# A list scheduler for everything ahead of the first exponential of a transformer layer

## The chip, the cores and the metric

The kernel runs on one core of a Trainium2 chip. The metric is the device time of one execution in microseconds; the value of a kernel is the median of its runs. Profiles show one execution each.

## The reference

The layer takes x (2048 rows of 512, f32), normalises its rows and adds three things: x itself, an attention block, and a dense block with a gelu.

```python
xn = layernorm(x)                                # rows of 512, eps 1e-5
qkv = (xn @ wqkv)                                # 512 x 1536; 32 heads of 16
p = softmax(q k^T * 16 ** -0.5)                  # 2048 x 2048 for each head
attention = (p @ v) @ wo
h = gelu(xn @ w1 + b1)                           # 512 x 1792
out = x + attention + h @ w2 + b2
```

## The kernel before, in words

Dense operands are carried as two f16 parts (a high part and the remainder of it), so that a product of 512 summands is twelve matmuls: four chunks of 128, each as high x high, high x low and low x high. The parts of a weight are made after scaling by a power of two, which needs the largest size of its entries: `scales` makes it from column maxima (or from absolute sums taken on ScalarE with `accum_out`) by a transpose, a row maximum, a broadcast matmul and a few small VectorE operations. This is called measuring a weight here. `w1`, `w2`, `wo` and the query and key columns of the later heads are loaded in pieces of 512 KB into the three buffers `wch` to be measured, and most of them loaded a second time later to be split.

The heads are worked in 8 groups of four. Queries and keys of a group are stored in DRAM (`qk_d`) from the tile `stg` and come back as stacks `qst` and `kst`, one for each block of 512 rows (four blocks), pair of heads and role; `stacks` issues the loads. Row block t of a group (32 row blocks in all) is 16 units. In each unit `s_half` computes four score tiles of 128 x 512 (matmuls into a PSUM bank `pS`, then `reduce_max` on VectorE, line 258); after 16 units the maxima go out to DRAM and come back as two more rows of the query stack (`s_end`, `store`). `LEAD` = 19 units later `e_half` computes the transposed scores with the maxima already subtracted (`pT`) and the exponential on ScalarE (line 303), and `v_half` multiplies by the values `vv` (`pV`). So the first exponential can only come when 19 score units are done: 16 for the first row block and three more. Beside the attention, `dense` fills TensorE with all other products (`pD`).

The loop over units (`unit`) starts from position `pos` and writes the order of every engine by hand (`manual_schedule`). Its work and the tail behind it are the same in both kernels. What lies ahead of it, the prologue, is in the kernel before written as generators that are advanced by hand: `stats` (row statistics and normalisation of four row tiles of x), `transpose_x` (transposes and the two f16 parts `xt`), `prep_qk` and `prep_v` (measuring and splitting the weights of head group 0..3 and of the values), `project` (queries or keys of four groups for one block of rows), `v_tiles` (the values of the first `NV` = 8 row tiles), `measure` (18 pieces, two of them by VectorE maxima at line 741, sixteen by absolute sums at line 857) and `tile_and_unit` (one unit of scores with some products of `v_tiles` between the halves). Only TensorE's order is fixed by hand there, from the transposes of the second block of x on; VectorE, ScalarE and the transfer queue (SP, which issues all DMAs) get the order of the program. The units 16 to 18 run in the loop already, with `LFILL` = (8, 16, 12) products of value tiles in place of the exponentials. Matmuls on a zeroed tile (`warm`, line 890) run at the start. `dbank` gives the dense products their PSUM bank; until unit `LEAD` it takes from the banks of `pT`.

PSUM has eight banks: three for scores (S), three for transposed scores (T), one for dense products (D), one for values (V). In the prologue transposes, projections and value tiles take turns on T, D, V and S.

After the prologue `rest` gives the dense work of the first stage (the remaining value tiles, then the projections of the other heads as soon as their weights are split), and `prepare` is advanced once in each unit: it ends the measuring (a reduction over the bias `b1_s`, the maxima over `am_all` and `amx`), and has the weights split on GpSimd.

Of the kernel before, what the change touches and what calls it, by code (L numbers as in the profile page):

```python
# [36 lines left out]
LFILL = (8, 16, 12)  # L37
WARM = (14, 3, 2, 2)
NV = 8
# [11 lines left out]
def layer_kernel(ctx: ExitStack, tc: tile.TileContext, x, wqkv, wo, w1, b1, w2, b2, out):  # L51
# [31 lines left out]
    def clear(i):  # L83
        for b in range(NQB):
# [120 lines left out]

    mt_of, ptiles, pv_of, stores = {}, {}, {}, {}
# [39 lines left out]
    def s_half(u, n):  # L246
# [4 lines left out]
        if t not in mt_of:  # L251
            mt_of[t] = work.tile([P, 4, 4, 4], F32, name="mt", bufs=2)
        ks, qs = kst[g % 2], qst[g % 2]
        p, a = divmod(n, 2)
        r = slice(64 * a, 64 * a + 62)
        s = banks("S")
        tiled(None, s, qs[p][qb][r, qt * P:(qt + 1) * P], ks[p][kb][r, :], True, True)
        nc.vector.reduce_max(mt_of[t][:, n, qt, kb:kb + 1], s, axis=AX.X)  # L258
        given("dve", 600)

# [145 lines left out]
    def dbank():  # L406
        turn[0] += 1
        if pos[0] < LEAD:
            return banks("T"), None
        return hold("D", "T")  # L410
# [46 lines left out]
    def split_qk(m, wf, inv, ready_w):  # L457
        wh = ph.tile([P, 2, 2, NC, P], F16, name="wqk_h", bufs=2)
        for w in (1, 0):
            split_pool(wh[:, w, 0], wh[:, w, 1], wf[w], inv[:, 8 + 2 * m + w:9 + 2 * m + w])  # L460
# [5 lines left out]
    def prep_qk(m, wf, bank, ready_w):  # L466
        am = work.tile([P, 2], F32, name="am_qk", bufs=2)
        for w in range(2):
            nc.vector.tensor_reduce(am[:, w:w + 1], wf[w], axis=AX.XY, op=ALU.max, apply_absolute_value=True)
            yield  # L470
        box = []
        yield from scales(am, 2, bank, box)
        inv, fac = box
        wh = ph.tile([P, 2, 2, NC, P], F16, name="wqk_h", bufs=2)
        for w in (1, 0):
            (split if w and m == 0 else split_pool)(wh[:, w, 0], wh[:, w, 1], wf[w], inv[:, w:w + 1])
            yield
        nc.vector.tensor_tensor(sexp[:, m:m + 1], fac[:, 0:1], fac[:, 1:2], op=ALU.mult)
        nc.vector.tensor_scalar_mul(sexp[:, m:m + 1], sexp[:, m:m + 1], DH ** -0.5)
        ready_w[m] = wh  # L480
# [179 lines left out]
    def unit(gen):  # L660
# [4 lines left out]
        if e >= 0 and e % (2 * NQB * 16) == 0 and e < NU:  # L665
            fetch_scale(e // (2 * NQB * 16))
        if u == LEAD and cur[0] is not None:
            burst(gen, cur[0].left())
        pos[0] += 1
        for a in range(2):  # L670
# [7 lines left out]
            if u < LEAD:  # L678
                burst(gen, LFILL[u - 16] // 2)
# [36 lines left out]
    with ExitStack() as st1:  # L716
# [6 lines left out]
        def load_x(t):  # L723
            xs[t] = px.tile([P, D], F32, name="xs", bufs=8)
            nc.sync.dma_start(xs[t], x[t * P:(t + 1) * P, :])

        def pin(i):
            if loads and not pos[0]:
                tc.keep_in_program_order(i)

        def chunk(src):
            wf = ph.tile([P, 4 * W], F32, name="wch", bufs=3)
            v = wf.rearrange("p (a b) -> p a b", b=src.shape[2])
            if len(loads) <= NM:
                pin(nc.sync.dma_start(v, src))
            else:
                later(2, lambda: nc.sync.dma_start(v, src), True)
            return v

        def absmax(dst, v):  # L740
            nc.vector.tensor_reduce(dst, v, axis=AX.XY if len(v.shape) == 3 else AX.X, op=ALU.max,
                                    apply_absolute_value=True)
            given("dve", 600)
# [11 lines left out]
        am_all = work.tile([P, 16], F32, name="am_all")  # L755
        fac1, inv1 = [], []

        def fetch(k):
            while len(loads) <= min(k + (1 if pos[0] else 2), NM + 15):
# [3 lines left out]
        for t in range(4):  # L763
            load_x(t)
        wfs.append(load_qk(0))
        for t in range(4, 8):
            load_x(t)
        wvv = wqkv[:, 2 * D:3 * D].rearrange("(c p) n -> p c n", p=P)
        loads = []
        wvf = [chunk(wvv[:, :, i * W:(i + 1) * W]) for i in range(2)]  # L770
        wvh = [ph.tile([P, NC, D], F16, name="wvh", tag="wsp", bufs=3) for _ in range(2)]
        fac_v, ready_w = [], {}

        def stats(sb):
            mv = work.tile([P, 4, nc.vector.BN_AGGR_DIM], F32, name="mv", bufs=2)
            for i in range(4):
                bs = work.tile([P, nc.vector.BN_STATS_DIM], F32, name="bs", bufs=2)
                nc.vector.bn_stats(bs, xs[4 * sb + i])
                yield
                nc.vector.bn_aggr(mv[:, i, :], bs)  # L780
            sd = work.tile([P, 5, 4], F32, name="sd", bufs=2)
            nc.vector.tensor_scalar_add(sd[:, 0], mv[:, :, 1], 1e-5)
            nc.scalar.activation(sd[:, 1], sd[:, 0], AF.Sqrt)
            yield

            nc.vector.tensor_scalar_mul(sd[:, 4], mv[:, :, 0], -1.0)
            nc.vector.tensor_tensor(sd[:, 2], sd[:, 1], sd[:, 1], op=ALU.mult)
            yield
            nc.vector.tensor_tensor(sd[:, 2], sd[:, 2], sd[:, 0], op=ALU.add)
            yield  # L790
            nc.vector.reciprocal(sd[:, 3], sd[:, 2])
            yield
            nc.vector.scalar_tensor_tensor(sd[:, 2], sd[:, 1], 2.0, sd[:, 3], op0=ALU.mult, op1=ALU.mult)
            yield
            for i in range(4):
                v = xs[4 * sb + i]
                if sb and i >= 2:
                    nc.scalar.activation(v, v, AF.Identity, bias=sd[:, 4, i:i + 1])
                    nc.scalar.activation(v, v, AF.Copy, scale=sd[:, 2, i:i + 1])
                else:  # L800
                    nc.vector.tensor_scalar(v, v, mv[:, i, 0:1], sd[:, 2, i:i + 1], op0=ALU.subtract, op1=ALU.mult)
                yield

        free = ["T", "D", "T", "V", "T", "S", "S"]

        def vbank():
            turn[0] += 1
            return banks(free[turn[0] % len(free)])

        def transpose_x(sb, c):  # L810
            cs = slice(sb * QB, (sb + 1) * QB)
            pt = vbank()
            for i in range(4):
                nc.tensor.transpose(pt[:, i * P:(i + 1) * P], xs[4 * sb + i][:, c * P:(c + 1) * P], ident)
            nc.scalar.activation(xt[:, 0, c, cs], pt, AF.Copy)
            if sb and c % 2:
                pf = ph.tile([P, QB], F32, name="pf", bufs=2)
                nc.scalar.activation(pf, pt, AF.Copy)
                nc.gpsimd.tensor_tensor(xt[:, 1, c, cs], pf, xt[:, 0, c, cs], op=ALU.subtract)
            else:  # L820
                nc.vector.tensor_tensor(xt[:, 1, c, cs], pt, xt[:, 0, c, cs], op=ALU.subtract)
            if c == NC - 1:
                for t in range(4 * sb + 8, min(4 * sb + 12, NT)):
                    load_x(t)

        def prep_v():
            am = work.tile([P, 3], F32, name="am_v")
            for i in range(2):
                junk = ph.tile([P, 4 * W], F32, name="wch", bufs=3)
                tc.keep_in_program_order(nc.scalar.activation(junk.rearrange("p (a b) -> p a b", b=W), wvf[i], AF.Abs,  # L830
                                                              scale=1.0 / SPREAD, accum_out=am[:, i:i + 1]))
                yield
            nc.vector.tensor_tensor(am[:, 2:3], am[:, 0:1], am[:, 1:2], op=ALU.max)
            box = []
            yield from scales(am[:, 2:3], 1, sbank, box)
            inv, fac = box
            fac_v.append(fac)
            for i in range(2):
                cs = slice(i * W, (i + 1) * W)
                split(wvh[0][:, :, cs], wvh[1][:, :, cs], wvf[i], inv[:, 0:1])  # L840

        def some(gen, n):
            for _ in range(n):
                next(gen, None)

        def measure():

            for w in range(2):
                v = fetch(w)
                for m in (2, 3):  # L850
                    absmax(am_all[:, 8 + 2 * m + w:9 + 2 * m + w], v[:, :, (m - 2) * P:(m - 1) * P])
                absmax(am_all[:, 10 + w:11 + w], wfs[1][w])
                yield
            for n in range(16):
                v = fetch(2 + n)
# [441 lines left out]
```

## Time and profile before

| what | us |
|---|---|
| median of three runs (lowest, highest) | 1510.72 (1508.43, 1512.08) |
| the profiled execution | 1512.14 |
| its span | 1510.4 |
| first score matmul, from the span's start | 38.80 |
| first exponential | 110.15 |
| TensorE, VectorE, ScalarE, GpSimd busy | 1479.5, 1385.1, 1258.9, 661.4 |

The page of the profile gives the busy time of each engine over the span. PE is TensorE, PEld its weight loads, DVE is VectorE, ACT is ScalarE, POOL is GpSimd, SP the queue that issues the transfers. In rows of the timeline stand the start, the length, the engine, the line of the kernel, the operation, the tile written and the tiles read, the count, and in brackets the idle time ahead of it with what ended that. In groups stand the count, busy time, mean in ns, and the idle time ahead of them by releaser. The chain of waits follows the work that ended last back to what released it.

### The profile page before, as it was taken

What the parts mean: (1) busy time and instruction counts of PE and PEld (TensorE: products, weight loads), DVE (VectorE), ACT (ScalarE), POOL (GpSimd) and SP (SyncE); (2) the same over time, 40 slices, a digit from 0 to 9 for tenths busy, and PEclk for the clock granted to TensorE, in tenths of its full rate; (3) what the DMA queues carried; (4) which work ended last, traced back from release to release, by engine and by line L of the source; (5) the groups of instructions that cost most, each with busy time, mean ns of one, the idle gap of its engine ahead of it and who ended that gap; (6) DMA issues with size and microseconds to landing.
All of it is one profiled execution on the core that took longest, in us unless ns stands there. A gap on an engine that the chain in (4) does not pass through costs nothing.

```text
span 1510.4 us, 87999 instructions
## 1 busy us (share of the span) xinstructions
PE 1479.5 (98%) x40052; PEld 820.6 (54%) x40052; DVE 1385.1 (92%) x2317; ACT 1258.9 (83%) x2351; POOL 661.4 (44%) x685
## 2 busy tenths in 40 slices
PE   7999999999999999999999999999999999999998
PEld 3435555555555555555555555555555555555553
DVE  7889998999899999999999999999999999999923
ACT  5548887888899888899988889998889999888884
POOL 3101879433577411268731137873104877211210
PEclk8999999999999999999999999999999999999999
DMA  7650676323322310131112211131111210111432
GB/s 227 182 182 26 206 236 208 109 75 104 88 75 74 91 50 29 40 79 43 50 40 58 53 43 41 42 85 57 29 34 53 70 43 20 50 53 39 131 97 93
DMA packets 114414, 124.82 MB, mean 83 GB/s; under 512 B 24700, under 2 KB 86012, under 8 KB 114040
## 3 DMA queue, kind: packets, MB, share of 16 engines
q1 hardware_dynamic: 114040, 119.19, 26.5%
q8 instruction: 313, 5.13, 1.4%
q14 instruction: 61, 0.50, 0.1%
HBM read 81.66 MB, written 37.34 MB: 79 GB/s over the span
## 4 chain that ended last, share of the span: by engine, by line
PE 78%; DVE 9%; DMA 4%; POOL 4%; SPq 2%; issue 1%; ACT 1%; DVEq 0%; POOLq 0%; ACTq 0%
PE pV L167 23%; PE pD L167 21%; PE pT L167 17%; PE pS L167 16%; DVE mt L258 8%; POOL wsp L1005 1%; DMA wch<-in_B_w_dram 1%; DMA qk_d<-stg 1%; POOL wch L1003 1%; DMA m_d<-mhl 1%; DMA wq<-in_A_wqkv_dram 1%; POOL wsp L1004 1%; SPq L402 1%; PE pT L436 0%; POOL stg L518 0%
## 5 line engine op out<-in xcount | busy, mean ns | idle before, releaser
L258 DVE TENSOR_REDUCE mt<-pS 128x1 f32<-128x512 f32 x2048 | 1307.4, 684 | 50.2 <-PE pS L167 30.5
L303 ACT ACTIVATE pe<-pT 128x512 f32<-128x512 f32 x2048 | 1111.9, 599 | 180.9 <-PE pT L167 77.3
L167 PE MATMUL pV<-pe,vv 64*32 64x512 f32 x8192 | 1077.9, 595 | 0.1
L167 PE MATMUL pT<-qst,kst 64*32 64x512 f16 x8192 | 714.3, 378 | 5.7 <-DMA qst<-m_d 4.2
L167 PE MATMUL pS<-kst,qst 62*32 62x512 f16 x8192 | 625.1, 379 | 7.3 <-DVE mt L258 4.7
L167 PEld LDWEIGHTS <-qst 62*32 62x32 f16 x8192 | 281.1, 92 | 226.5 <-issue 59.4
L167 PEld LDWEIGHTS <-kst 64*32 64x32 f16 x8192 | 280.7, 91 | 178.4 <-issue 77.3
L167 PE MATMUL pD<-xb,wc 64*32 64x512 f16 x5376 | 362.2, 378 | 0.0
L167 PE MATMUL pD<-w_s,g 64*32 64x512 f16 x5376 | 359.4, 377 | 0.0
L167 PEld LDWEIGHTS pV<-pe,vv 64*32 64x32 f32 x8192 | 183.4, 105 | 88.5 <-PE pV L167 2.9
L167 PE MATMUL pD<-xt,wqk_h 64*32 64x512 f16 x2304 | 152.2, 378 | 0.1
L167 PEld LDWEIGHTS <-wc 64*32 64x32 f16 x5376 | 117.6, 92 | 42.9 <-issue 0.6
L167 PEld LDWEIGHTS <-g 64*32 64x32 f16 x5376 | 113.3, 92 | 43.8
L1139 POOL TENSOR_TENSOR xa<-xa,yt 128x512 f32<-128x512 f32 x16 | 20.4, 1278 | 242.0 <-ACT yt L1137 241.9
L359 POOL TENSOR_TENSOR osb<-osb,rb 128x512 f32<-128x512 f32 x31 | 40.0, 1289 | 171.6 <-DMA rb<-den_d 151.1
L1094 POOL TENSOR_TENSOR t<-hh 128x512 f32<-128x512 f32 x56 | 58.3, 1042 | 78.4 <-ACT hh L1114 77.4
L1096 POOL TENSOR_TENSOR t<-t,hh 128x512 f32<-128x512 f32 x56 | 71.9, 1284 | 4.7
L1089 POOL TENSOR_TENSOR t<-t,hh 128x512 f32<-128x512 f32 x56 | 71.8, 1281 | 4.7
L1091 POOL TENSOR_TENSOR g<-t,g 128x512 f16<-128x512 f32 x56 | 65.2, 1164 | 4.7
L1088 POOL TENSOR_SCALAR t<-t,gs 128x512 f32<-128x512 f32 x56 | 39.0, 696 | 55.1 <-ACT t L1083 54.8
L167 PEld LDWEIGHTS <-wqk_h 64*32 64x32 f16 x2304 | 52.2, 92 | 19.7 <-issue 2.2
L167 PE MATMUL pD<-wo_s,oc 64*32 64x512 f16 x732 | 48.5, 378 | 0.0
(145 smaller groups left out, 871.0 us busy)
## 6 DMA issues: line engine op xcount, KB each, us to landing
wch<-in_B_w_dram SPq DMA_DIRECT2D x28, 512.0 KB
wc<-w_d SPq DMA_DIRECT2D x56, 256.0 KB
qk_d<-stg SPq DMA_DIRECT2D x32, 256.0 KB
rb<-den_d SPq DMA_DIRECT2D x124, 64.0 KB
w_d<-wsp SPq DMA_DIRECT2D x28, 256.0 KB
kst<-qk_d SPq DMA_DIRECT2D x128, 48.0 KB
qst<-qk_d SPq DMA_DIRECT2D x128, 48.0 KB
xs<-in_A_x_dram SPq DMA_DIRECT2D x16, 256.0 KB
```

What stands on the lines that cost most here:

```text
L167: p = nc.tensor.matmul(*args, **kw)
L258: nc.vector.reduce_max(mt_of[t][:, n, qt, kb:kb + 1], s, axis=AX.X)
L303: nc.scalar.activation(pe, st, AF.Exp, scale=scale_of[g // 2])
L359: pooled((1280, lambda: nc.gpsimd.tensor_tensor(osb, osb, rb, op=ALU.mult)), (620, lambda: nc.gpsimd.tensor_scalar(ot[:, 0], osb, 1.0, 0.0 ...
L402: nc.sync.dma_start((qst, kst)[w][g % 2][p][b][64 * a:64 * a + 48, :], qk_d[w, h * DH:(h + 1) * DH, :, b * QB:(b + 1) * QB].rearrange("d j ...
L1003: pooled((1240, lambda: nc.gpsimd.tensor_scalar(src, src, inv, 0.0, op0=ALU.mult, op1=ALU.add)), (1240, lambda: nc.gpsimd.tensor_scalar(hi ...
L1088: pooled((690, lambda: nc.gpsimd.tensor_scalar(t1, t1, 1.0, gs[:, 1:2], op0=ALU.add, op1=ALU.mult)), (1280, lambda: nc.gpsimd.tensor_tenso ...
L1089: (1280, lambda: nc.gpsimd.tensor_tensor(t1, t1, hh, op=ALU.mult)),
L1091: (1160, lambda: nc.gpsimd.tensor_tensor(g[:, 1, f, :], t1, g[:, 0, f, :], op=ALU.subtract)),
L1094: pooled((1040, lambda: nc.gpsimd.tensor_tensor(t1, hh, hh, op=ALU.mult)), (620, lambda: nc.gpsimd.tensor_scalar(t1, t1, 1.0, 1.0 / GELU_A ...
L1096: (1280, lambda: nc.gpsimd.tensor_tensor(t1, t1, hh, op=ALU.mult)),
L1139: add = lambda: nc.gpsimd.tensor_tensor(xa, xa, yt, op=ALU.add)
```

## The change

All work ahead of the first exponential becomes a list of tasks (`Plan.add`: engine, estimated ns, function, the tasks it comes after, the pool slots it takes and frees, KB of a transfer). `Plan.run` first gives each task a tail, the longest estimated way from it to the end, and then emits tasks one by one: of the engine that can start earliest, the task with the longest tail among those that can start within 120 ns of it. Every queue (TensorE, ScalarE, VectorE, GpSimd, SP) is kept in the order of emission. Estimates of the hand-over between engines are in `LATE`; a transfer is counted as 1300 ns, 3 ns for each KB on one shared wire, and 500 ns.

```diff
+    class Plan:
+        LATE = {"PE": 280, "ACT": 180, "DVE": 150, "POOL": 150, "SP": 0}
...
+        def run(self, fill):
+            for t in reversed(self.todo):
+                for a in t["after"]:
+                    wire = 1800 + a["size"] * 3 if a["size"] else 0
+                    a["tail"] = max(a["tail"], t["tail"] + max(t["ns"] + self.late(a, t) + wire, t["gap"] if a["gap"] else 0))
...
+            while left:
+                can = {}
+                for t in left:
+                    s = self.start(t, at[t["e"]])
+                    if s is not None:
+                        can.setdefault(t["e"], []).append((s, t))
+                first = {e: min(s for s, t in c) for e, c in can.items()}
+                e = min(first, key=first.get)
+                s, t = max((c for c in can[e] if c[0] <= first[e] + 120), key=lambda c: (c[1]["tail"], -c[1]["n"]))
+                if e == "PE":
+                    fill(at[e], s)
...
+        ctx.enter_context(tc.manual_schedule(engines=ORDERED))
+        plan = Plan(xs=8, stg=3, pf=2, wch=3, wq=2, S=4, X=4)
...
+        def sb_tile(key):
+            return bank_tile((0, 1, 2, 7)[plan.slot[key]], "SSSV"[plan.slot[key]])
...
+        def piece_in(key, src, after=()):
+            def fn():
+                tl[key] = raw(key, "wch", [P, 4 * W], 3).rearrange("p (a b) -> p a b", b=src.shape[2])
+                nc.sync.dma_start(tl[key], src)
+            return add("SP", 420, fn, after, take=[key], size=700)
+
+        def total(ns, key, dst, after, done=()):
+            def fn():
+                v = tl[key]
+                o = v if done else junk[:, :v.shape[1] * v.shape[2]].rearrange("p (a b) -> p a b", b=v.shape[2])
+                nc.scalar.activation(o, v, AF.Abs, scale=1.0 / SPREAD, accum_out=dst)
+            return add("ACT", ns, fn, [after], free=done)
...
+                old = m_prev[-4:-2]
+                s_prev[0] = add("PE", 450, mm, [s_prev[0]] + k_ready[kb] + q_ready[t] + old, take=keys, gap=1230)
+                for key in keys:
+                    m_prev.append(add("DVE", 607, lambda key=key: s_max(key[1], key[2], tl[key]), [s_prev[0]], free=[key]))
...
+        def v_tile(t):
...
+            add("ACT", 480, fn, [p], free=[key], tail=VT[0] * (NV - t) + VT[1])
...
+        hot = work.tile([P, 1], F32, name="hot")
+        add("ACT", 1400, lambda: nc.scalar.activation(hot, ident[:, 0:1], AF.Exp), n_last)
+        def low(t):
+            t["tail"] = -20000
...
+        for n, src in enumerate(every[:NM]):
+            key = ("wch", "m", n)
+            dst = am_all[:, 12 + n:13 + n] if n < 2 else am_all[:, n - 2:n - 1] if n < 9 else amx[:, n - 2:n - 1]
+            low(total(1150, key, dst, piece_in(key, src, k_ready[1]), done=[key]))
+
+        def fill(a, b):
+            if b - a > 700 and not s_of:
+                for _ in range(int((b - a - 250) / WARM)):
                     nc.tensor.matmul(wp, wvh[0][:, 0, 0:P], wvh[0][:, 0, :], start=True, stop=True)
...
+        plan.run(fill)
         nc.sync.dma_start(b1_s, b1.rearrange("(f p) -> p f", p=P))
-        pos[0] = 16
+        pos[0] = LEAD
```

What else differs:

- The units 16 to 18 of the scores, the eleven value tiles (`NV` 8 to 11, `VT` their tails) and the store of the first maxima are tasks of the plan; the loop starts at `LEAD` with the first exponential. `LFILL` and the branch of `dbank` for it are gone.
- In the plan scores use four banks (the three of S and that of V), everything else four (the three of T and that of D).
- The weights of head group 0 to 3 and all 18 pieces are measured by absolute sums on ScalarE; the VectorE maxima of `prep_qk` and `absmax` are gone. The heads of the last two column blocks share one scale (`min(m, 2)`, `am_all` of 14 columns).
- Normalising two row tiles of the first two blocks each stays on VectorE; the other twelve go to ScalarE, in one instruction with scale and bias where there were two. The remainders of `xt` are VectorE's for the first two blocks and GpSimd's for the last two (`DVE_X`, `DVE_LO`). For the keys and for the queries of the first block, VectorE takes the remainder of a projection.
- Pieces are issued after the second key block is stacked (`k_ready[1]`), with a tail of their sums below all others.
- `hot`, an exponential of one column, stands behind the last square root; the first scale of the exponential is read into a register there too.
- `clear(1)` is split in four and put into the plan; `b1_s` is loaded behind the plan, where before it stood in the program ahead of the loop without a fixed place in SP's order.

More of the change, by code (lines that the diff above doesn't have):

```diff
@@ L81, in layer_kernel, with clear @@
                  for i in range(2)] for x in "kq")
-    def clear(i):
-        for b in range(NQB):
+    def clear(i, blocks=range(NQB)):
+        for b in blocks:
             for p in range(2):
@@ L464, in split_qk @@
             later(4, lambda: wfs.append(load_qk(m + 1)), True)
[L466 to L480, printed above, removed]
     def by_slots(gen):
@@ L826, in prep_v @@
[L826 to L855, printed above, removed]
-                dst = am_all[:, n:n + 1] if n < 7 else amx[:, n:n + 1]
-                pin(nc.scalar.activation(v, v, AF.Abs, scale=1.0 / SPREAD, accum_out=dst))
-                yield
@@ new lines, in twelve, with fn @@
+        def twelve(key, prods, ready):
+            last = None
+            for c in range(NC):
+                def fn(c=c):
+                    if c == 0:
+                        xbank(key)
+                    for n in range(3):
+                        lhs, rhs = prods[3 * c + n]()
+                        nc.tensor.matmul(tl[key], lhs, rhs, start=c + n == 0, stop=(c, n) == (NC - 1, 2))
+                last = add("PE", 650, fn, ready(c) + [last], take=[key] if c == 0 else [])
+            return last
@@ new lines, in layer_kernel @@
+        chain, inv_v, fv = scale_chain(amv[:, 2:3], 1, [a], "v")
+        fac_v.append(fv)
+        wv_ready = []
+        for i in range(2):
+            hi, lo = (wvh[j][:, :, i * W:(i + 1) * W] for j in range(2))
+            key = ("wch", "v", i)
+            h = add("ACT", 1040, lambda hi=hi, key=key: nc.scalar.activation(hi, tl[key], AF.Copy, scale=inv_v[:, 0:1]), [chain])
+            wv_ready.append(add("DVE", 1200, lambda hi=hi, lo=lo, key=key: nc.vector.scalar_tensor_tensor(
+                lo, tl[key], inv_v[:, 0:1], hi, op0=ALU.mult, op1=ALU.subtract), [h], free=[key]))
```

462 lines of the change are left out of this document (275 added, 187 removed).

## The prediction

> **What bounds the kernel now.** I read the page first, then the busy time by stage, then the chain of waits around the first exponential, and last the groups and the timeline up to there. Of the page:
>
> ```profile
> PE 1479.5 (98%) x40052; PEld 820.6 (54%) x40052; DVE 1385.1 (92%) x2317; ACT 1258.9 (83%) x2351; POOL 661.4 (44%) x685
> ```
>
> TensorE counts as busy nearly throughout, but a matmul that is spread out or runs at half clock counts as busy too, so the stages decide. Columns: stretch, then busy us and instructions of TensorE, its weight loads, VectorE, ScalarE and GpSimd, then clock, DMA share and GB/s.
>
> ```profile
> 0.00:28.00 28.00, 18.04 (x71) 9.69 (x72) 21.84 (x69) 12.32 (x23) 12.02 (x44) 0.89 0.76 223
> 28.00:38.80 10.80, 10.57 (x40) 5.20 (x38) 6.85 (x13) 6.83 (x11) 2.32 (x2) 0.64 0.75 234
> 38.80:95.20 56.40, 53.95 (x443) 21.70 (x443) 49.54 (x89) 29.72 (x56) 8.12 (x7) 0.99 0.61 183
> 95.20:110.15 14.95, 13.39 (x127) 4.99 (x126) 9.68 (x23) 8.05 (x13) 0.00 (x0) 0.93 0.65 211
> 300.00:320.00 20.00, 20.00 (x612) 11.66 (x604) 19.32 (x32) 17.24 (x33) 3.58 (x4) 1.00 0.22 67
> ```
>
> After the first exponential (300 to 320 stands for it) TensorE and VectorE are both full, 20.00 and 19.32 of 20. That part takes 1400 us, and the change leaves its work alone. Before it there is slack: VectorE does 9.68 in the last 14.95, and the DMA share is 0.61 to 0.76. So what can be won is the time of the first exponential. What leads there, from the chain of waits (start, us, what):
>
> ```profile
> 91.17 4.04 DMA wch<-in_B_w_dram
> 95.29 1.16 ACT wch L857 x2
> 96.47 3.63 DMA wch<-in_A_wo_dram
> 100.18 1.16 ACT wch L857 x2
> 101.52 0.61 DVE mt L258
> ...
> 108.86 1.28 ACT L303
> 110.15 0.61 ACT pe L303
> ```
>
> Weight pieces are measured one behind the other (a load, then an absolute sum on ScalarE); a row maximum stands behind the last of them in VectorE's order, score and value matmuls behind that, and a table load of 1.28 us directly ahead of the first exponential at 110.15. That is order, not load.
>
> **The change, part by part.** The list scheduler emits everything up to score unit 18, all DMAs included, and every queue then runs in that order. At the first exponential both kernels have done the same: 19 score units (76 maxima), 8 projections of head group 0, 11 value tiles (8 and the 36 products of the fill before; 11 by plan after), 18 measured pieces. The loop starts from the same point, so the sum needs one number, X, the new time of the first exponential. Groups up to 110.15, then the timeline (start, length, what, count):
>
> ```profile
> L258 DVE TENSOR_REDUCE mt<-pS 128x1 f32<-128x512 f32 x79 | 48.7, 681 | 1.3 <-PE pS L167 0.9 <-PE pT L167 0.2
> ...
> L741 DVE TENSOR_REDUCE am_all<-wch 128x1 f32<-128x512 f32 x4 | 2.6, 680 | 1.1 <-DMA wch<-in_A_wqkv_dram 1.1
> ```
>
> ```profile
> 12.19 0.47 PE L814 MATMUL pD<-ident,xs 128*128 128x128 f32 x1 [1.16 <-DVE xs L801]
> 17.28 0.50 SPq L972 DMA_DIRECT2D b_s<-in_B_b_dram  x1
> 24.29 0.69 DVE L509 TENSOR_TENSOR stg<-pS,stg 128x512 f16<-128x512 f32 x1
> 27.68 1.70 SPq L402 DMA_DIRECT2D qst<-qk_d  x4
> 31.35 7.51 PE L436 MATMUL pT<-xt,wqk_h 128*128 128x512 f16 x24
> 38.80 0.41 PE L167 MATMUL pS<-kst,qst 62*32 62x512 f16 x8
> 48.14 0.60 PE L814 MATMUL pT<-ident,xs 128*128 128x128 f32 x4
> 53.57 5.34 PE L436 MATMUL pT<-xt,wqk_h 128*128 128x512 f16 x24
> 79.70 15.62 DVE L258 TENSOR_REDUCE mt<-pS 128x1 f32<-128x512 f32 x26
> 80.91 0.51 PE L167 MATMUL pS<-kst,qst 62*32 62x512 f16 x8
> 81.36 0.82 PE L436 MATMUL pD<-wvh,xt 128*128 128x512 f16 x3
> 82.11 0.51 PE L167 MATMUL pS<-kst,qst 62*32 62x512 f16 x8
> ...
> 124.01 1.16 POOL L150 TENSOR_TENSOR wqk_h<-wq,wqk_h 128x512 f16<-128x512 f32 x1
> ```
>
> *First score.* Now at 38.80. Its last stack loads were issued by 29.4 (27.68 + 1.70). A landing takes about 2.1 us, as this row of the chain of waits has it:
>
> ```profile
> 59.26 2.12 DMA qk_d<-stg
> ```
>
> So the data were there at 31.5, and the scores stood behind 24 projection matmuls that end at 38.86: 7.3 us of pure order. Earlier, the remainder at 24.29 had stood behind statistics and weight maxima on VectorE. In the plan scores have the longest tail and go first, and the eight weight maxima (L741's four, four more on the 256 KB tiles, 8 x 0.68 = 5.4 us) leave VectorE. So 31.5 less 0 to 6; I take 28, bounds 25 and 33 (33 if the first blocks meet the rows of x still loading).
>
> *TensorE.* A score pair and three value products alternate every 82.11 - 80.91 = 1.20 us: 0.45 for the pair, 0.75 for the three. A run of 24 projection matmuls costs 5.34, 0.22 each; four transposes 0.60. So 38 pairs x 0.45 = 17.1; 44 value triples x 0.75 = 33.0; 96 projection matmuls x 0.22 = 21.1; 16 sets of transposes x 0.60 = 9.6; sum 80.8. In runs without changes of kind the values cost 132 x 0.22 = 29.0, and transposes no more than before: 77. The first useful matmul stands at 12.19 and waits for row statistics, which the change keeps. So X is 89 at the least and 93.0 at today's interleaved prices.
>
> *VectorE.* 26 maxima take 15.62, 0.60 each; 76 take 45.6. The rest of VectorE up to 110.15 is 21.84 + 6.85 + 49.54 + 9.68 = 87.9, less 48.7 of maxima, less 5.4 = 34. Some 22 of it runs before 28, as the first stage does today. 28 + 45.6 + 12 = 86: nearly the bound, not quite.
>
> *Pieces.* The instructions of the sums, first and last start:
>
> ```profile
> L857 ACT ACTIVATE wch<-wch x16: 1045/1056/1072, 44.1 to 100.2; 128x1024 f32<-128x1024 f32 x16
> ```
>
> All 18 sums precede the first exponential in ScalarE's order. They cost it 18 x 1.16 = 21, and it is busy only 56.9 of 110.15 today; what counts is their data. Pieces are issued after the second key block is stacked, some 7 us behind the first: 35. Best case: a share of 0.61 at 183 GB/s makes 300 GB/s when full, so 1.75 us for 512 KB and 31 for 18, and 15 for the 4.5 MB of other transfers behind it (five projections of 576 KB out and back, 1.5 MB of inputs): 81. Worst case, today's pace, (100.2 - 44.1) / 15 = 3.74: 35 + 67 + 1 = 103. I take the middle, 2.9 a piece: 88, hidden by TensorE, because buffers come free by ScalarE's own list and no longer by the tile loop.
>
> *Warm matmuls, table.* Warm matmuls fill planned gaps of TensorE ahead of the scores; the clock of 0.64 from 28 to 38.8 shows what they can save, at most 0.36 x 10.8 = 3.9 us, and where a gap turns out shorter than planned they cost 0.4 each. I take zero. A dummy exponential loads the table in a gap of ScalarE: 1.28 us leaves the path, and X contains that. The Trainium skill ("ScalarE: Activation LUTs", What ACT_TABLE_LOAD costs) gives a set switch 2.66 us, drain included. The trace puts the exponential 0.01 us behind a load of 1.28, so no drain shows; by the page X would be 1.4 us lower.
>
> *X.* 12.2 + 80.8 = 93.0, plus 2 for waits that no other work covers (bounds -4, from the runs, and +10, where the pieces end last): **X = 95**, 15.15 earlier than 110.15.
>
> *Behind X.* The bias load, issued at 17.28 now, stands behind the whole plan in the transfer queue, and VectorE reads it at the end of the first loop unit, with the next maxima queued behind. Between 0 and 2.1 (one landing); I take 1. `prepare` starts three units later against X; a unit is four maxima, 2.4 us, so 7.2. Today the split for the next heads ends at 125.2, and its first product stands here:
>
> ```profile
> L167 PE MATMUL pD<-xt,wqk_h x2304: 372/376/388, 149.8 to 350.8; 64*32 64x512 f16 x192
> ```
>
> Five value tiles cover 24 us, so nothing; uncovered, 7 us of products would slide to the end. A shifted loop may meet its transfers otherwise; no row shows that, ±2.
>
> **The sum.** The profiled execution took 1512.14, span 1510.4 and 1.7 around it: 1512.14 - 15.15 + 1 = 1498.0. It lies 1.4 above the median of 1510.72, so for a median **1497**.
>
> **The rivals.**
>
> *A, the forecast: TensorE's own work sets X, 87 to 101*, median 1488.5 to 1502.5. For it: the other engines' sums lie below. Chance 0.66.
>
> *B, the pieces keep today's pace:* X = 101 to 106, median 1502.5 to 1507.5. For it: three buffers then as now. Against it: some of the pace is the tile loop's. Chance 0.18.
>
> *C, the new order is worth no more than the old* (a late key block, VectorE late with a remainder): X = 107 to 113, within 3 us of today; 3 us, 0.2%, is about what a measurement of this kernel can tell from no change. Against it: 7.3 us of order at the first score alone. Chance 0.06.
>
> *D, slower: ScalarE blocks on late pieces.* Its list is in order; a sum that waits for a load holds the evictions behind it, TensorE's banks fill, projections come late, and with them the stores that stand ahead of the next pieces. It happens once today:
>
> ```profile
> 83.75 0.82 PE L436 MATMUL pD<-wvh,xt 128*128 128x512 f16 x3
> ...
> 90.00 1.06 ACT L857 ACTIVATE wch<-wch 128x1024 f32<-128x1024 f32 x1 [9.30 <-DMA wch<-in_B_w_dram]
> ...
> 91.06 0.58 ACT L536 ACTIVATE vv<-pD 128x512 f32<-128x512 f32 x1
> ```
>
> The value tile that ended at 84.6 was evicted at 91.06, since ScalarE stood 9.30 us for a piece. A load and its sum in line take 3.63 + 1.16 = 4.79 (at 96.47). If all 18 stood so: 35 + 86 + 1 = 122, median 1523.5. It decides from (110.15 - 1 - 35) / 18 = 4.1 us a piece on. Against it: three loads in flight, and the plan counts 2.1 us of transfer for each against 1.75 above, so it errs to the late side. The Trainium skill ("TensorE: Matmul & The Clock Gate", Architectural detail: the array is 16× 32×32, not 1× 128×128) calls the queues of ScalarE and VectorE strict FIFO, which is what this needs; the eviction at 91.06 agrees. Chance 0.10.
>
> **How the numbers follow.** Faster by over 0.2%: A, B and 0.02 of C, 0.86. Same: the rest of C, 0.04. Slower: D, 0.10. The range goes from A's lower end to B's upper end, **1488 to 1508**, and leaves out C and D, 0.16.
>
> **What would show it.** First exponential at 87 to 101 with no table load ahead of it; first score at 25 to 33; from 28 on score pairs and value triples in turn with no wait of TensorE over 2 us; last sum on ScalarE before 92, 18 of them under 3.2 us apart; from the first exponential to the end 1400 ± 3. I am wrong if the last sum comes after 101 with ScalarE waiting for loads (B, D), if the first score comes after 35, or if the loop's part is longer by over 4 us (the bias load or `prepare` uncovered).

## The result and the profile after

The changed kernel takes 1509.11 us (median; lowest 1505.92, highest 1519.1) where the kernel before, run beside it, takes 1510.78. The ratio is 0.9998 with a 95% interval of 0.9984 to 1.0011: no difference that can be measured. (It is the ratio of the two means, 1510.31 and 1510.68; that of the two medians is 0.9989.) 1497 was forecast, with a range of 1488 to 1508, and faster with 0.86. The profiled execution took 1507.74, its span is 1506.0.

Yet the part ahead of the loop went nearly as forecast. Of the page of the changed kernel:

```profile
PE 1475.0 (98%) x40055; PEld 814.7 (54%) x40055; DVE 1376.2 (91%) x2306; ACT 1266.5 (84%) x2367; POOL 662.8 (44%) x687
```

The busy time by stage of the changed kernel, with the stretches of the prediction and three short ones around the first exponential behind them:

```profile
0.00:28.00 28.00, 23.17 (x97) 12.41 (x98) 20.49 (x62) 17.38 (x33) 12.26 (x44) 0.88 0.73 228
28.00:38.80 10.80, 8.90 (x60) 3.86 (x60) 8.01 (x18) 7.53 (x13) 2.00 (x2) 0.84 0.57 186
38.80:95.20 56.40, 55.03 (x466) 21.13 (x458) 44.75 (x86) 39.88 (x74) 9.47 (x10) 1.00 0.64 197
95.20:110.15 14.95, 11.03 (x201) 4.77 (x203) 10.55 (x21) 5.49 (x10) 1.14 (x2) 0.77 0.46 115
300.00:320.00 20.00, 20.00 (x612) 11.22 (x597) 19.14 (x32) 16.95 (x33) 7.18 (x9) 1.00 0.19 57
95.00:100.00 5.00, 1.94 (x32) 0.51 (x36) 4.29 (x8) 0.00 (x0) 1.34 (x2) 0.87 0.40 137
100.00:105.00 5.00, 5.00 (x88) 2.50 (x93) 2.53 (x4) 2.47 (x5) 0.00 (x0) 0.50 0.42 80
105.00:110.00 5.00, 3.97 (x97) 1.65 (x88) 3.79 (x10) 2.87 (x6) 0.00 (x0) 0.95 0.54 117
```

From 38.8 to 95.2 TensorE is full (55.03 of 56.40, clock 1.00), as the plan meant. Then it does 1.94 in five microseconds, next 88 matmuls at half clock, and then 3.97 of five. ScalarE does nothing at all from 95 to 100. The timeline of the changed kernel shows what is waited for:

```profile
32.84 0.70 PE L167 MATMUL pS<-kst,qst 62*32 62x512 f16 x12 [1.39 <-DMA qst<-qk_d]
43.98 1.06 ACT L847 ACTIVATE wch<-wch 128x1024 f32<-128x1024 f32 x1
...
86.64 1.05 ACT L847 ACTIVATE wch<-wch 128x1024 f32<-128x1024 f32 x1
90.31 1.47 PE L958 MATMUL pT<-xt,wqk_h 128*128 128x512 f16 x6
90.38 0.22 DVE L1072 TENSOR_REDUCE mneg<-mt 128x16 f32<-128x64 f32 x1
...
92.05 1.47 PE L958 MATMUL pT<-xt,wqk_h 128*128 128x512 f16 x6
...
93.67 0.22 PE L1081 MATMUL pS<-ident,mneg 64*32 64x64 f32 x1
...
94.75 0.22 DVE L1086 SCALAR_TENSOR_TENSOR mhl<-pS,mhl 64x64 f16<-64x64 f32 x1
94.99 0.67 SPq L1088 DMA_DIRECT2D m_d<-mhl  x1
95.75 0.52 SPq L984 DMA_DIRECT2D qk_d<-stg  x1
96.33 0.56 SPq L1088 DMA_DIRECT2D m_d<-mhl  x1
...
98.22 1.22 SPq L1093 DMA_DIRECT2D qst<-m_d  x4
99.20 0.61 PE L167 MATMUL pS<-kst,qst 62*32 62x512 f16 x4 [1.99 <-DVE mt L330]
99.48 3.57 SPq L990 DMA_DIRECT2D qst<-qk_d  x8
99.91 0.65 PE L167 MATMUL pT<-qst,kst 64*32 64x512 f16 x8
100.58 1.09 ACT L381 ACTIVATE pe<-pT 128x512 f32<-128x512 f32 x2 [5.61 <-PE pT L167]
103.09 0.42 SPq L1127 DMA_DIRECT2D b_s<-in_B_b_dram  x1
106.21 0.17 DVE L1165 TENSOR_REDUCE am_all<-b_s 128x1 f32<-128x14 f32 x1 [2.19 <-DMA b_s<-in_B_b_dram]
```

The first score comes at 32.84 instead of 38.80, the last of the 18 sums at 86.64 instead of 100.2, the first exponential at 100.58 instead of 110.15. Two places spoil it.

*The chain of the first maxima.* The sixteen row maxima are complete at 90.38. From there to the first exponential lie 10.2 us of steps one behind the other: 3.3 in which their transpose (L1081, 93.67) stands in TensorE's order behind two groups of six projection products; 1.3 to the split and the first store (94.99); 1.3 to the second store (96.33), between which a store of a projection has its turn; 1.9 until it has landed (98.22); 1.7 for the four loads into the query stack (99.91); 0.7 for the first product. The plan had given most of TensorE's work out by then.

*The bias.* Its load stands in SP's order behind eight query stacks (99.48, 3.57 us of issuing), is issued at 103.09 and lands 3.1 later, as the chain of waits has it (start, us, what), with the store of the maxima on the same chain:

```profile
96.33 1.87 DMA m_d<-mhl
...
103.09 3.10 DMA b_s<-in_B_b_dram
```

VectorE stands 2.19 at 106.21 for it, with the maxima of the loop's units queued behind and TensorE's banks behind those.

### The profile page after: what moved, and what is told of

Same layout as the page of the kernel before. It is cut to its first block, busy times and chain, and to the rows that moved or that the text cites. A ratio compares the mean times of both kernels' runs of the same rounds, so it can differ in the third digit from the quotient of the medians.

```text
span 1506.0 us, 87998 instructions
## 1 busy us (share of the span) xinstructions
PE 1475.0 (98%) x40055; PEld 814.7 (54%) x40055; DVE 1376.2 (91%) x2306; ACT 1266.5 (84%) x2367; POOL 662.8 (44%) x687
## 2 busy tenths in 40 slices
DMA packets 114414, 124.82 MB, mean 83 GB/s; under 512 B 24700, under 2 KB 86012, under 8 KB 114040
## 4 chain that ended last, share of the span: by engine, by line
PE 86%; DVE 8%; DMA 3%; issue 1%; ACT 1%; SPq 1%; DVEq 0%; ACTq 0%
PE pV L167 25%; PE pD L167 22%; PE pS L167 18%; PE pT L167 18%; DVE mt L330 7%; PE pT L958 2%; DMA m_d<-mhl 1%; DMA xs<-in_A_x_dram 1%; PE pD L958 1%; DVE ac L1326 0%; PE pT L928 0%; DMA qst<-m_d 0%; DVE bs L896 0%; DVE mneg L347 0%; SPq L990 0%
## 5 line engine op out<-in xcount | busy, mean ns | idle before, releaser
L167 PE MATMUL pS<-kst,qst 62*32 62x512 f16 x8116 | 617.8, 379 | 9.2 <-DVE mt L330 6.1
L167 PEld LDWEIGHTS <-qst 62*32 62x32 f16 x8192 | 277.9, 92 | 230.5 <-issue 58.9
```

Source lines behind the costliest of these rows:

```text
L167: p = nc.tensor.matmul(*args, **kw)
```

## Experiments

The ratio is that of each kernel to the kernel before, run beside it; X is the first exponential in the kernel's own profiled execution. The theories as they are named in the expectations: 1, the chain of the first maxima is uncovered and the bias is waited for; 1a, the half clock behind the gap; 2, the rival to theory 1 in each run (VectorE's backlog of maxima slows the first units; in cover_chain and cover_and_bias, TensorE's own sum sets X at 99.5 or later); 5, VectorE or the chain of maxima sets X and not TensorE's work; 3, the gain is there and scatter hides it; 4, the late bias load itself, 1792 packets of 4 bytes, disturbs other transfers.

| kernel | ratio, 95% interval | median | X | clock, 28 to 38.8 | exponentials by 150 |
|---|---|---|---|---|---|
| changed | 0.9998 [0.9984, 1.0011] | 1509.11 | 100.58 | 0.84 | 68 |
| changed_again | 0.9987 [0.9974, 1.0] | 1508.04 | 101.22 | 0.84 | 68 |
| bias_early | 0.9963 [0.9949, 0.9977] | 1505.68 | 101.23 | 0.84 | 68 |
| bias_not_read | 0.9997 [0.9982, 1.0012] | 1508.71 | 98.15 | 1.00 | 73 |
| bias_not_read_2 | 0.9969 [0.9954, 0.9984] | 1507.22 | 100.69 | 0.84 | 69 |
| bias_twice | 0.9974 [0.996, 0.9987] | 1508.42 | 98.30 | 1.00 | 72 |
| warm_joint | 0.9999 [0.9984, 1.0014] | 1510.66 | 101.05 | 0.84 | 63 |
| cover_chain | 0.9996 [0.9982, 1.0009] | 1511.0 | 94.92 | 1.00 | 67 |
| cover_and_bias | 0.9943 [0.9921, 0.9965] | 1503.25 | 94.96 | 1.00 | 79 |
| cover_and_bias_2 | 0.9930 [0.9914, 0.9946] | 1500.55 | 97.30 | 0.84 | 74 |
| cover_and_bias_twice | 0.9927 [0.9904, 0.995] | 1500.02 | 94.79 | 1.00 | 80 |
| values_twice | 0.9974 [0.9959, 0.999] | 1508.12 | 101.97 | 1.00 | 68 |

The last three columns are of one execution each (the kernel before has 62 exponentials by 150). The changed kernel, its repeat and the two of bias_not_read have the same code up to the loop, yet X is 98.15 in the execution with a granted clock of 1.00 from 28 to 38.8 and 100.58 to 101.22 in the three with 0.84. The busy time by stage there, of the changed kernel first and of bias_not_read behind it (the clock is the third number from the end):

```profile
28.00:38.80 10.80, 8.90 (x60) 3.86 (x60) 8.01 (x18) 7.53 (x13) 2.00 (x2) 0.84 0.57 186
28.00:38.80 10.80, 8.82 (x82) 3.86 (x85) 9.62 (x19) 8.38 (x14) 3.47 (x3) 1.00 0.55 163
```

What makes that clock differ is not shown. So X is to be compared at the same clock: covering the chain moves it from 98.15 and 98.30 to 94.79 to 94.96 at 1.00, and from 100.58 to 101.23 to 97.30 at 0.84, by 3.2 to 3.9 us.

**The bias load as a task of the plan** (bias_early): it goes out behind the last rows of x, ahead of the pieces.

```diff
+        add("SP", 420, lambda: nc.sync.dma_start(b1_s, b1.rearrange("(f p) -> p f", p=P)), [x_in[NT - 1]], size=7)
         hot = work.tile([P, 1], F32, name="hot")
...
         plan.run(fill)
...
-        nc.sync.dma_start(b1_s, b1.rearrange("(f p) -> p f", p=P))
```

> The changed kernel with one edit: the bias load is a task of the plan behind the last tile of x, no longer issued behind the whole plan. Theory 1 (the first units of the loop lose time because VectorE stands for the bias, 2.19 us in the changed kernel, and TensorE behind it at half clock): first exponential unchanged at 100.6, no VectorE wait for the bias, the exponentials are 6 to 7 us ahead of the kernel before at 120 us in place of 4; time 2 to 3 us below the changed kernel, ratio to the kernel before 0.995 to 0.997. Theory 2 (the early units are slow because VectorE still has the maxima of units 16 to 18 to do, the bias wait only fills a hole): first exponential and lead as in the changed kernel, ratio 0.997 to 1.000.

Faster: 0.9963. In its profile the reduction over the bias no longer waits. But this execution has no more exponentials by 150 than the changed kernel (68), and at 120 it is 8 of them (5.4 us) ahead of the kernel before, where 6 to 7 us were expected. The gap ahead of the first exponential and the half clock stay as they were, as its busy time by stage shows:

```profile
95.00:100.00 5.00, 1.89 (x24) 0.52 (x23) 4.62 (x10) 0.48 (x1) 1.84 (x2) 0.92 0.45 156
100.00:105.00 5.00, 4.76 (x80) 2.20 (x84) 2.90 (x8) 2.17 (x4) 0.00 (x0) 0.50 0.33 86
105.00:110.00 5.00, 5.00 (x132) 2.65 (x130) 4.44 (x8) 3.42 (x7) 0.00 (x0) 0.90 0.56 164
```

From 105 to 110 TensorE is now full, where it did 3.97.

**Warm matmuls at the joint** (warm_joint): nine matmuls on the zeroed tile between plan and loop, in a bank that is free there.

```diff
         plan.run(fill)
...
+        wj = bank_tile(6, "D")
+        for _ in range(9):
+            nc.tensor.matmul(wj, wvh[0][:, 0, 0:P], wvh[0][:, 0, :], start=True, stop=True)
         pos[0] = LEAD
```

> The changed kernel with nine matmuls of 128x512 on a free bank between plan and loop (about 2 us at full clock), where TensorE stood 1.99 us. Theory 1a (the half clock from 100 to 105 us, 88 matmuls in place of about 160, comes from the TensorE gap ahead of it and costs 2 us or more): granted clock 1.00 in 100 to 105, lead over the kernel before at 120 us up by 2 us, ratio 0.995 to 0.997. Theory 2 (early units wait for VectorE and transfers, the clock only fills the wait): clock up, first exponential up to 1 us later, time unchanged or worse, ratio 0.998 to 1.001.

No gain: 0.9999. The busy time by stage shows why:

```profile
100.00:105.00 5.00, 3.80 (x100) 2.04 (x101) 2.65 (x4) 3.71 (x7) 0.00 (x0) 1.00 0.34 82
105.00:110.00 5.00, 1.83 (x32) 0.73 (x31) 2.69 (x7) 0.70 (x2) 0.00 (x0) 0.64 0.56 103
```

The clock is whole from 100 to 105, the matmuls there are done sooner, and TensorE then stands from 105 to 110 (1.83 busy). VectorE waits 3.77 for the bias there, and X is 101.05. With the bias as late as ever, the half clock only filled a wait. So 1a falls as a cause by itself, as far as a comparison with an interval of 0.0015 either way can tell.

**Cover for the chain** (cover_chain): the last two value tiles, and the projections of query blocks 2 and 3, get shorter tails. So the last scores go first, and this work is what TensorE does while the maxima are stored and come back.

```diff
+            for t in self.todo:
+                t["tail"] -= t.get("shift", 0)
...
-            add("ACT", 480, fn, [p], free=[key], tail=VT[0] * (NV - t) + VT[1])
+            add("ACT", 480, fn, [p], free=[key], tail=VT[0] * (NV - t) + VT[1] - (25000 if t >= 9 else 0))
...
+        n_q = len(plan.todo)
         q_ready[2] = project0(0, 2)
         q_ready[3] = project0(0, 3)
+        for t in plan.todo[n_q:]:
+            t["shift"] = 12000
```

The first two lines stand in `run`, behind the loop that gives the tails.

> The changed kernel with the last two value tiles and the last two query projections pushed down in the plan, so that the last scores go ahead of them and they stand beside and behind the store of the first maxima. Theory 1 (the first exponential comes 6.7 us after TensorE's own work, because nothing covers the store of the first maxima): the row maxima are reduced at about 87 to 88 in place of 90.4 and stored at once; first exponential at 96 to 98 in place of 100.6; VectorE still waits for the bias, even longer, so the time falls by 0 to 3 us, ratio 0.995 to 0.999. Theory 2 (the sum of TensorE's work or the weight pieces set the first exponential): first exponential 100 to 101 as before, no gain.

X moves to 94.92, where the forecast had put it and below the 96 to 98 that was expected (at clock 1.00, so 3.2 to 3.4 of the move are the cover's). The time does not move: 0.9996, above the 0.995 to 0.999 of theory 1. Its timeline:

```profile
89.88 1.24 SPq L1090 DMA_DIRECT2D m_d<-mhl  x1
...
94.92 3.09 ACT L383 ACTIVATE pe<-pT 128x512 f32<-128x512 f32 x6
...
97.57 4.76 SPq L992 DMA_DIRECT2D qst<-qk_d  x8
...
102.38 0.42 SPq L1132 DMA_DIRECT2D b_s<-in_B_b_dram  x1
...
105.63 0.17 DVE L1170 TENSOR_REDUCE am_all<-b_s 128x1 f32<-128x14 f32 x1 [8.69 <-DMA b_s<-in_B_b_dram]
```

and of its busy time by stage:

```profile
100.00:105.00 5.00, 0.00 (x0) 0.00 (x0) 0.00 (x0) 0.00 (x0) 0.00 (x0) 0.76 0.47 74
```

The stores of the maxima go out 6 us earlier and the loop starts earlier, but the bias is issued only 0.7 earlier (102.38 against 103.09), since it is held behind the query stacks, and those come behind the stores of the projections that the cover put off. VectorE waits 8.69 us for it, and from 100 to 105 all five engines stand.

**Both** (cover_and_bias, and once more as cover_and_bias_2): the two edits together.

> Both edits: bias load early, and the last value tiles and query projections behind the last scores. Theory 1 (chain uncovered, then the bias wait): first exponential 96 to 98, lead over the kernel before at 120 us 8 to 10 us, time 5 to 7 us below the changed kernel, ratio 0.992 to 0.995. Theory 2 (TensorE's sum sets the first exponential, VectorE's backlog the first units): first exponential above 99.5, ratio 0.997 to 1.000.

> cover_and_bias once more, for a second profile and on the chip of the three others; the first had a ratio of 0.9943 from six runs, while its profile was the fastest of them. Theory 1: first exponential 95, ratio 0.994 to 0.996, and the profile shows a lead of 15 to 18 exponentials (0.65 us each) over the kernel before at 150 us; whatever is lost against 15 us is lost in single waits between 200 and 400 us. Theory 3: the time falls by 13 us as in the first profile, ratio 0.991 to 0.992.

0.9943 and 0.9930. Against the kernel before, the cover alone brings nothing that can be measured and the early bias 0.4% (0.2% as the mean of four measurements without the wait, below); together they bring 0.6 to 0.7%. The numbers of the second expectation did not come: its ratio lies between the ranges of theories 1 and 3, X is 97.30 (at clock 0.84), and the lead at 150 is 12 exponentials and not 15 to 18. The busy time by stage of cover_and_bias, where the changed kernel had its gap:

```profile
95.00:100.00 5.00, 5.00 (x141) 2.62 (x136) 4.79 (x12) 4.27 (x10) 1.48 (x2) 1.00 0.46 156
100.00:105.00 5.00, 5.00 (x154) 2.90 (x146) 4.54 (x9) 3.95 (x8) 0.00 (x0) 1.00 0.33 82
```

TensorE is full, at clock 1.00, straight through the joint. With its median of 1500.55 to 1503.25 this version beats both kernels.

**What sets X then** (values_twice): in the kernel with both edits two value tiles are computed a second time, 24 more products on TensorE and their evictions on ScalarE.

```diff
-        def v_tile(t):
-            key = ("X", "v", t)
+        def v_tile(t, again=0):
+            key = ("X", "v", t, again)
...
         for t in range(NV):
             v_tile(t)
+        for t in (7, 8):
+            v_tile(t, 1)
```

The flag `again` tells the second copy of a tile from the first in the plan.

> Early bias load and covered chain as in cover_and_bias (first exponential 94.96, ratio 0.9943), and two value tiles computed twice in the plan: 24 matmuls of 512 columns, 5.2 us of TensorE and two evictions. Theory 1 (TensorE's own work sets the first exponential): first exponential 99.5 to 100.5, time 5 us above cover_and_bias, ratio 0.997 to 0.999. Theory 5 (VectorE or the chain of the row maxima sets it, TensorE has room): first exponential 95 to 97, time up to 2 us above, ratio 0.994 to 0.996.

X goes to 101.97, from 94.96 and 97.30 in the two profiles without the extra products, and the ratio to 0.9974, 6.6 us above cover_and_bias_2 beside which it ran (0.0044 of 1510). 24 products are some 5.3 to 6 (0.22 to 0.25 each, as in the prediction's sum). X is above the 99.5 to 100.5 of theory 1, because the first score also came late in this execution, at 33.23; from the first score to X it is 68.7, against 62.9 from 32.01 in cover_and_bias, so 5.8 more. The busy time by stage of values_twice:

```profile
38.80:90.00 51.20, 50.47 (x413) 20.06 (x405) 37.45 (x73) 37.10 (x68) 7.94 (x7) 1.00 0.71 218
90.00:100.00 10.00, 10.00 (x92) 3.38 (x86) 9.69 (x19) 1.78 (x4) 0.00 (x0) 1.00 0.02 4
```

VectorE has 13.7 of 51.2 free up to 90 and no more work than before, and from 90 to 100 both are full. A shift by the price of the added products is what theory 1 asks for and theory 5 does not; TensorE's own work sets X, once the chain is covered.

**The bias loaded late but not read** (bias_not_read and its repeat; the bias is left out of the largest sizes):

```diff
-            nc.vector.tensor_reduce(am[:, 7:8], b1_s, axis=AX.X, op=ALU.max, apply_absolute_value=True)
+            nc.vector.memset(am[:, 7:8], 0.0)
```

> The changed kernel, whose bias load stays behind the whole plan, but the reduction over the bias in the first loop unit is replaced by a memset of its column (the bias is left out of the measuring), so nobody waits for the load before the dense block reads it at about 360 us. Theory 1 (the wait costs): ratio like that of the early bias load, 0.995 to 0.997. Theory 4 (not the wait but the load costs, 1792 packets of 4 bytes in the transfer queue while stacks and row maxima pass): ratio 0.999 to 1.001, as the changed kernel.

> The late bias load stays, the reduction that reads it at the start of the loop is a memset; the bias is left out of the measuring of the gelu's scale. Repeat. If the wait for the bias costs the time, the ratio to the kernel before is 0.995 to 0.997 as with the bias load early, and 0.9997 in the first run was scatter of this program; if the late load itself costs it (theory 4), the ratio is 0.998 to 1.000 again.

**An unread second load in the old place** (bias_twice on bias_early, cover_and_bias_twice on cover_and_bias):

```diff
         plan.run(fill)
...
+        b2_s = const.tile(list(b1_s.shape), F32, name="b2_s")
+        nc.sync.dma_start(b2_s, b1.rearrange("(f p) -> p f", p=P))
```

> The bias is loaded early, as a task of the plan, and is read from there; behind the plan, where the changed kernel loads it, the same load goes into a tile that nobody reads. Wait theory: as with the early load alone, ratio 0.995 to 0.998. Theory 4 (the load of 1792 small packets disturbs the transfers behind it): ratio 0.998 to 1.000, as the changed kernel.

> The same unread second load, in the kernel with covered store chain and early bias. Wait theory: ratio 0.992 to 0.995, as without it. Theory 4: 0.996 to 0.999.

The first run of bias_not_read, 0.9997, spoke for the load and not the wait. The repeat, 0.9969, does not, and neither do the two kernels with the load in its late place and nobody waiting: 0.9974 and 0.9927, as without it. Theory 4 falls; it is the wait, as far as anything is lost here. The two runs of bias_not_read, 0.9997 and 0.9969, have intervals that only just touch, and so show how much one of these ratios can be off: about 0.0015 either way.

**The change once more** (changed_again, unedited):

> The changed kernel, nothing edited, beside the others on one chip and with a second profile. Theory 1 (its lead of 9.6 us at the first exponential falls to about 4 us while VectorE waits for the bias, whose landing differs from execution to execution): ratio 0.998 to 1.000; in the second profile first exponential again at 100 to 101, VectorE's wait for the bias between 2 and 6 us. Theory 3 (the lead lasts, and the median hides it by noise of the later stages): ratio 0.996 to 0.997, bias wait as in the first profile.

0.9987, its interval ending at 1.0. X is 101.22 and VectorE waits 1.71 for the bias, both a little outside what was expected (100 to 101, 2 to 6). With 0.9998 the mean is 0.9992, about 1 us faster than before. Theory 3 holds in so far as this microsecond is below what one comparison can tell; it doesn't hold for the forecast 14.

## Why the prediction was wrong, step by step

*First score at 28 (25 to 33):* 32.84, at the upper bound. It waited 1.39 for a query stack.

*TensorE's work, 12.2 + 80.8 = 93.0, and X = 95:* the mechanism is right. TensorE is full from 38.8 to 94, and its work sets X as soon as nothing else does: 94.79 to 97.30 with the chain covered, against the forecast 95. That the total fits so well is in part luck. In cover_and_bias TensorE is busy 79.27 of the 82.70 from 12.20 to 94.90, some 1.7 of it with warm matmuls and 0.5 with the loop's first products. So the planned work took about 77, the lower of my two prices, and waits and warm matmuls took the rest.

*Pieces, 2.9 us each, the last at about 88:* right in substance, (86.64 - 43.98) / 17 = 2.5 us apart in the mean, the last sum at 86.64 (single gaps go up to 7.3, from 46.17 to 53.50, where I had named 3.2). In the groups of the changed kernel up to 110 ScalarE's waits for them are:

```profile
L847 ACT ACTIVATE wch<-wch 128x1024 f32<-128x1024 f32 x18 | 19.0, 1061 | 2.2 <-DMA wch<-in_B_w_dram 1.9 <-DMA wch<-in_A_wo_dram 0.2
```

2.2 us in all, so rivals B and D did not happen. C's time came out, but by none of the causes that it named.

*"Plus 2 for waits that no other work covers":* **the first step that failed.** I put the upper bound of 10 on late pieces, and did not follow the first maxima through the plan: transpose, split, two stores, landing, loads, 10.2 us in line, with nothing left to cover them. Covering them is worth 3.2 to 3.9 of X at the same clock. X = 100.58 is 5.6 above the forecast; the other 2.4 or so go with the half clock of this execution (0.50 from 34 to 36, where that of bias_not_read, at X = 98.15, had 1.00). My sum priced TensorE's work at full clock and took zero for the warm matmuls. Rival A's range for X, up to 101, took 100.58 in; its time did not, for what follows.

*The table load, "1.28 us leaves the path, and X contains that":* counted too high, by 1.2 at most. In the kernel before, the loop's first products ran beside that load. Of the timeline of the kernel before:

```profile
108.25 0.60 PE L167 MATMUL pT<-qst,kst 64*32 64x512 f16 x8
...
110.80 0.40 PE L167 MATMUL pT<-qst,kst 64*32 64x512 f16 x4 [0.87 <-ACT pe L303]
```

TensorE began the loop there at 108.25 and ran on while ScalarE loaded its table; in the changed kernel it begins at 99.91. So the start of the loop moved by 8.3 and X by 9.6, 1.2 more (unrounded). But the row at 110.80 shows that TensorE then stood 0.87 for the first exponential, so most of the load was on its path after all; I estimate that 0.4 to 1.2 was not. The Trainium skill ("ScalarE: Activation LUTs", What ACT_TABLE_LOAD costs) counts a drain of 1.38 to such a load. The timeline of the changed kernel, where the dummy exponential carries it, shows none:

```profile
50.91 1.28 ACT L1104 ACT_TABLE_LOAD   x1
52.20 0.20 ACT L1104 ACTIVATE hot<-ident 128x1 f32<-128x1 f32 x1
```

The exponential follows 0.01 behind the 1.28.

*"The bias load ... I take 1", bounds 0 and 2.1:* **the second step that failed.** I bounded it by one landing, and left out that SP's order holds its issue behind eight query stacks, and that it takes 3.10 to land where the store of the maxima took 1.87. What this costs depends on X. With the chain uncovered VectorE stands 2.19 (1.71 in the repeat). The four measurements in which nobody waits and the chain is as in the change (0.9963, 0.9997, 0.9969, 0.9974) have a mean of 0.9976, the two of the change 0.9992: 2.5 us, give or take some 2 by their intervals. By 150 us the executions at clock 0.84 have 68 and 69 exponentials without the wait and 68 and 68 with it, one more at most, 0.7 us. So it is not shown that the wait alone is beyond my bounds. At the X that I forecast it is: in cover_chain, at 94.92, VectorE stands 8.69, and taking the wait away is worth 0.9996 - 0.9933 (the mean of the three), 9.5 us, or 12 to 13 exponentials by 150 (67 against 79 and 80), 8 to 9 us. So an X of 95 and a wait of 1 could not both come. The two waits overlap: each hides what the other costs, and so the cover alone gained nothing.

*`prepare` three units later:* the first product for the next heads stands at 144.9 in the changed kernel, where it stood at 149.8. No wait of TensorE between 115 and 200 is over 0.7 us there, and it is busy 83.75 of these 85 us (84.86 before), so 1.1 at most hangs on it.

*The sum.* X gave 5.6, the loop 1506.0 - 100.58 = 1405.4 instead of 1400.25 + 1, another 4.2: together the 9.7 between 1498.0 and 1507.74. So the loop's part is 5.2 longer than today's 1400.25, beyond the 4 that I had named as a sign of being wrong. Of the 4.2, the table is at most 1.2 and the bias beyond the 1 that was taken at most some 1.5; 1.5 or more stays open. The rest of the way to the median is which execution was profiled: that of before lay 1.4 above the median I was given, that of the change 1.4 below its own. The count of exponentials shows that the lost part is lost at the start and stays lost:

| exponentials done by | 115 | 200 | 1450 |
|---|---|---|---|
| before | 10 | 132 | 1988 |
| changed | 16 | 138 | 1995 |
| cover_and_bias | 28 | 148 | 2006 |
| cover_and_bias_2 | 26 | 145 | 1996 |

In the kernel before, one comes every (1450 - 200) / (1988 - 132) = 0.67 us. So of 9.6 us the change has 6 x 0.67 = 4.0 left by 115, and keeps it. The last line shows what else scatters: cover_and_bias_2 is 2 behind cover_and_bias at 115 and 10 behind at 1450, and 7 of these come between 200 and 260 (221 against 231 by 260). There TensorE waits 1.7 us for the maxima of a later row block, which it does not in cover_and_bias; at 365 to 390 it waits for them in both and in both kernels of the comparison, 3.3 to 4.5 us. Which execution meets such waits where was not settled.

## What to carry to other kernels

A scheduler that orders by the longest way to the end still leaves the last chain bare if the filler has gone out before it: follow the final chain step by step through every queue, transfers included, and keep back enough independent work to cover it. A small load moved to the end of a queue costs the queue ahead of it as well as its landing, and what waits on it is every instruction behind its reader. When two waits lie side by side, taking away either one can show nothing; take away both before calling the gain absent. And before two executions are compared, see whether their clocks agree: here the same code came to its first exponential 2.4 to 3.1 us apart.

## What the hardware showed

A second load of the 1792 numbers of the bias, 7 KB, adds 1808 packets to the page (116222 in cover_and_bias_twice, 114414 in cover_and_bias), so about one for each number. Such a load took 3.10 us to land where the store of the maxima took 1.87; how much of that is its packets and how much the eight stack loads ahead of it, no run takes apart. Unread, it cost its neighbours nothing that can be measured (0.9927 with it, 0.9930 and 0.9943 without). After the five microseconds with 1.94 of matmuls the granted clock was 0.50 for the next five and 0.95 after that. The Trainium skill ("TensorE: Matmul & The Clock Gate", Part 1: The HAM clock gate (the "warmup" mystery)) has half rate after an idle window of some 3.4 us; the trace agrees with the half rate, but the longest idle time of TensorE between 38.8 and there is 1.99 (the row at 99.20), so no stand of that length went ahead of it. Here the half clock cost nothing that can be measured by itself: with a whole clock and the bias late as ever, the ratio was 0.9999. From 34 to 36 a clock of 0.50 went with a later X, as told above.
